# A gated attention and gMLP mixer on one core: w_phi loaded block-diagonal, and the first two tiles' matmuls by column halves

## The chip, the cores and the metric

The kernel runs on one core of a Trainium2 chip. The metric is device time in microseconds (us); lower is better. All times below are us unless marked ns. Engines are called by the profile's names: PE (TensorE matmul), PEld (its weight loads), DVE (VectorE), ACT (ScalarE), POOL (GpSimd) and SP (SyncE, which here only issues DMAs). A "q" behind a name (SPq, ACTq) is that engine's own queue of instructions that issue DMAs.

## What is computed

x is [2048, 512] in bf16. Two branches are mixed by a gate per row. Cut to what matters:

```python
g = sigmoid((x * gate_w).sum(-1, keepdims=True))
# branch A: linear attention, 32 heads of 16
q, k, v = split(x @ wqkv)
pq, pk = q @ w_phi[h], k @ w_phi[h]                     # per head, 16 x 16
phi = concat(softmax(p), softmax(-p))                   # for pq and pk
kv, z = phi_k.T @ v, phi_k.sum(0)                       # per head
a = ((phi_q @ kv) / (phi_q @ z + 1e-6)) @ wo
# branch B: gMLP
zz = gelu(x @ w_in)                                     # [2048, 1376]
z1, z2 = zz[:, :688], layernorm(zz[:, 688:])
b = (z1 * (w_sp @ z2 + b_sp[:, None])) @ w_out
out = g * a + (1 - g) * b
```

## The kernel before

Rows of x are handled in 16 tiles of 128. x transposed, xT, is the stationary operand of nearly all first-stage matmuls; its 512 rows are four blocks of 128, called dt = 0 to 3.

**The stages.** (1) For each tile, z2 = gelu(x @ w_in[:, 688:]) and z1 = gelu(x @ w_in[:, :688]): eight matmuls for each, four dt blocks by two column halves j of 344 (z_mm, L201; z_one, L193). z2_tile also makes the gate's logit: gate_w stands as one more column, column 688 of w_z2, so that half j=1 has 345 columns. z2_norm (L269) normalizes z2 four tiles at a time. The order by chunks c of four tiles is z2 of the chunk, then z1 of the chunk. In chunks c=2 and c=3 `fold` (L315) multiplies w_phi into the key part and the query part of wqkv; it reads wqkT (wqkv transposed) and wphi, a block-diagonal [128, 4, 128] image of w_phi with eight 16x16 heads to a 128-column block. (2) Then, tile by tile, keys, values, the kv sum, and w_sp @ z2 (gg_half, L460), with queries between them. (3) Attention output and the last products with wo and w_out (L500 to L505), and the stores.

**What sets the order.** PE and ACT run in the order in which the program is written (manual_schedule, L336). DVE, POOL and SP are ordered by the planner. Each engine takes its queue strictly in order. A DMA issue from SP or ACT is an instruction of that queue. The DMAs of both share eight completion marks in turn, so the ninth DMA in program order, and each one after it, is issued only when the DMA eight places earlier has landed.

**The start.** SP loads the rows of tiles 0 and 1 (xs, L122 and L124), block dt=2 of w_z2, and the rows of tiles 2 and 3 in one DMA (L129). ACT loads blocks dt=0 and dt=1 of w_z2, the gate row, and block dt=3. POOL issues the DMA of the bias row b_sp (brow, L118). Then SP issues w_z1 in two DMAs (L132), six DMA transposes of x for tiles 4 to 15 (L135, L137), w_phi into 16 partitions (wphiE, L140), the DMA transpose of the query and key parts of wqkv (L141), the value part (wv_sb, L142), and four DMA transposes of w_sp (L147).

`z2_first_two` (L219) writes out by hand what PE does first. It begins with matmuls of constants (warm_up, L224) into a buffer that is overwritten later. `x_T(i, d0, d1, ...)` (L282) transposes blocks of xs on PE into a PSUM buffer called pq, and DVE (or ACT) copies them to xT. `one(tt, dt, j)` is one z2 matmul of tile 0 or 1. `gate_T` (L292) turns the gate row into a column with one small matmul into a pq buffer, and a DVE copy puts it into w_z2's column 688; all matmuls of half j=1 wait for it. There are two pq buffers, taken in turn (pq_tile, L190), and three zp buffers (zp_tile, L187), in which z1 and z2 accumulate. `b_T` (L297) does with the bias row what gate_T does with the gate row; its result bT is first read by gg_half's DVE instruction (L468). `wphi_fold` (L302) builds wphi: four PE matmuls spread wphiE by the 0/1 matrix eexp, and DVE multiplies by the mask mask_bd. eexp and mask_bd are made on POOL (L151 to L164).

Of the kernel before, what the change touches and what calls it, by code (L numbers as in the profile page):

```python
# [8 lines left out]
ALU = mybir.AluOpType  # L9
AX = mybir.AxisListType  # L10
FP32 = mybir.dt.float32
BF16 = mybir.dt.bfloat16
I32 = mybir.dt.int32

P = 128
S = 2048
D = 512
H = 32
DH = 16
F = 1376  # L20
FH = 688
HF = FH // 2
NT = S // P
NDT = D // P
# [11 lines left out]
def kernel(  # L36
# [14 lines left out]
    nc = tc.nc  # L51
# [6 lines left out]
    early = early_cm.__enter__()  # L58
# [5 lines left out]
    w_z2 = early.tile([P, NDT, WP], BF16, name="w_z2")  # L64
    wv_sb = kvw.tile([P, NDT, D], BF16, name="wv_sb")
# [3 lines left out]
    z2all = pers.tile([P, NT, FH], BF16, name="z2all")  # L69
    z1all = pers.tile([P, NT, FH], BF16, name="z1all")  # L70
    wqkT = early.tile([P, 8, D], BF16, name="wqkT")
    wphiE = early.tile([P, H, DH], BF16, name="wphiE")
    eexp = early.tile([P, P], BF16, name="eexp")
    wphi = early.tile([P, NDT, P], BF16, name="wphi")
    mask_bd = early.tile([P, P], BF16, name="mask_bd")
    mask64 = pers.tile([P, NG, DH], BF16, name="mask64")
    mask4 = pers.tile([P, NG], BF16, name="mask4")
    kvz = pers.tile([P, 8, AW], BF16, name="kvz")
# [16 lines left out]
    gaterow = early.tile([P, P], BF16, name="gaterow")  # L95
    brow = early.tile([P, P], BF16, name="brow")
    zeros = early.tile([P, 32], BF16, name="zeros")

    w_in_v = B_w_in.rearrange("(dt p) f -> p dt f", p=P)
# [7 lines left out]
        out=ramp[:, 0, :], data0=ones32[:, :], data1=zeros[:, :], initial=0.0,  # L107
# [4 lines left out]
    for q in range(4):  # L112
        qs = slice(32 * q, 32 * q + 32)
        nc.vector.tensor_tensor(
            out=ident[qs, qs], in0=ramp[qs, 0, :], in1=ramp[qs, 1, :], op=ALU.is_equal)
    nc.gpsimd.memset(brow[:], 0.0)
    nc.gpsimd.memset(wphiE[:], 0.0)
    nc.gpsimd.dma_start(out=brow[0:NT, :], in_=B_b_sp.rearrange("(t p) -> t p", p=P))  # L118
    def load_z2w(eng, dt):
        eng.dma_start(out=w_z2[:, dt, 0:FH], in_=w_in_v[:, dt, FH:F])  # L120

    nc.sync.dma_start(out=xs[:, 0, :], in_=x2[0:P, :])  # L122
    load_z2w(nc.scalar, 0)
    nc.sync.dma_start(out=xs[:, 1, :], in_=x2[P:2 * P, :])  # L124
    load_z2w(nc.scalar, 1)
    load_z2w(nc.sync, 2)
    nc.scalar.dma_start(out=gaterow[0:NDT, :], in_=gate_w.rearrange("(dt p) -> dt p", p=P))
    load_z2w(nc.scalar, 3)
    nc.sync.dma_start(  # L129
        out=xs[:, 2:4, :], in_=x2[2 * P:4 * P, :].rearrange("(i p) d -> p i d", p=P))  # L130
    for h in range(2):
        nc.sync.dma_start(  # L132
            out=w_z1[:, 2 * h:2 * h + 2, :], in_=w_in_v[:, 2 * h:2 * h + 2, 0:FH])
    for i in range(4, 8):
        nc.sync.dma_start_transpose(out=xT[:, :, i * P:(i + 1) * P], in_=x2[i * P:(i + 1) * P, :])  # L135
    for q in range(2, NCH):
        nc.sync.dma_start_transpose(  # L137
            out=xT[:, :, q * CH:(q + 1) * CH], in_=x2[q * CH:(q + 1) * CH, :]
        )
    nc.sync.dma_start(out=wphiE[0:DH, :, :], in_=A_w_phi.rearrange("h e f -> e h f"))  # L140
    nc.sync.dma_start_transpose(out=wqkT[:, :, :], in_=A_wqkv[:, 0:2 * D])  # L141
    nc.sync.dma_start(  # L142
        out=wv_sb[:, :, :],
        in_=A_wqkv[:, 2 * D:3 * D].rearrange("(dt p) n -> p dt n", p=P),
    )
    for q in range(NCH):
        nc.sync.dma_start_transpose(  # L147
            out=wspT[:, :, q * CH:(q + 1) * CH], in_=B_w_sp[q * CH:(q + 1) * CH, :]
        )
    nc.gpsimd.memset(mhalf[:], -0.5)  # L150
    nc.gpsimd.memset(eexp[:], 0.0)  # L151
    nc.gpsimd.affine_select(
        out=eexp[:, :], in_=eexp[:, :], pattern=[[0, 8], [-1, 16]],
        compare_op=ALU.not_equal, fill=1.0, base=0, channel_multiplier=1,
    )
    nc.gpsimd.memset(mask_bd[:], 1.0)
    nc.gpsimd.affine_select(
        out=mask_bd[:], in_=mask_bd[:], pattern=[[-16, 8], [0, 16]],
        compare_op=ALU.is_ge, fill=0.0, base=0, channel_multiplier=1,
    )  # L160
    nc.gpsimd.affine_select(
        out=mask_bd[:], in_=mask_bd[:], pattern=[[16, 8], [0, 16]],
        compare_op=ALU.is_ge, fill=0.0, base=15, channel_multiplier=-1,
    )  # L164
    nc.gpsimd.memset(mask4[:], 1.0)
    nc.gpsimd.affine_select(
        out=mask4[:], in_=mask4[:], pattern=[[-32, NG]],
        compare_op=ALU.is_ge, fill=0.0, base=0, channel_multiplier=1,
    )
    nc.gpsimd.affine_select(  # L170
        out=mask4[:], in_=mask4[:], pattern=[[32, NG]],
        compare_op=ALU.is_ge, fill=0.0, base=31, channel_multiplier=-1,
# [17 lines left out]
    def pq_tile(shape, dtype=FP32):  # L190
        return psF.tile(shape, dtype, name="pq", tag=next_turn("pq", 2))
# [16 lines left out]
    def z2_out(tt, zp):  # L208
        z2v = z2all[:, tt, :].rearrange("p (j n) -> p j n", j=2)
        nc.scalar.activation(out=z2v, in_=zp[:, :, 0:HF], func=AF.Gelu_apprx_tanh)  # L210
        nc.vector.tensor_copy(out=glog[:, tt:tt + 1], in_=zp[:, 1, HF:HF + 1])
        for j in range(2):
            nc.vector.bn_stats(out=bn6[:, tt, j, :], in_=z2v[:, j, :])  # L213
        nc.vector.bn_aggr(out=mv[:, tt, :], in_=bn6[:, tt, :, :].rearrange("p j s -> p (j s)"))
# [4 lines left out]
    def z2_first_two():  # L219
        zps = [zp_tile() for _ in range(2)]  # L220
        tp1 = psA.tile([P, 2, P], BF16, name="tp1", tag=next_turn("zp", 3))
        turn["zp"] -= 1

        def warm_up(n, w=CH):  # L224
            for _ in range(n):
                nc.tensor.matmul(
                    zps[0][:, 1, 0:w], lhsT=nc.const_aps.tensor(1.0, [P, P], BF16),
                    rhs=nc.const_aps.tensor(1.0, [P, w], BF16), start=True, stop=True)

        def one(tt, dt, j):  # L230
            z_one(zps[tt], tt, w_z2, FH + 1, dt, j)

        warm_up(6)
        warm_up(5, P)
        x_T(0, 0, 1, pq_tile([P, 1, P], BF16)[:, :, :])
        x_T(0, 1, NDT, pq_tile([P, 3, P], BF16)[:, :, :], on_act=True)
        warm_up(3, P)
        one(0, 0, 0)
        x_T(1, 0, 2, tp1[:, :, :])
        x_T(1, 2, NDT, pq_tile([P, 2, P], BF16)[:, :, :], on_act=True)  # L240
        one(0, 1, 0)
        warm_up(2, P)
        one(1, 0, 0)
        one(1, 1, 0)
        gate_T()
        one(0, 2, 0)
        one(1, 2, 0)
        for dt in range(2):
            one(0, dt, 1)
            one(1, dt, 1)  # L250
        one(0, 2, 1)
        one(1, 2, 1)
        x_T(2, 0, NDT, pq_tile([P, NDT, P], BF16)[:, :, :])
        one(0, 3, 0)
        one(0, 3, 1)
        z2_out(0, zps[0])
        one(1, 3, 0)
        one(1, 3, 1)
        z2_out(1, zps[1])
        x_T(3, 0, NDT, pq_tile([P, NDT, P], BF16)[:, :, :])  # L260

    def z1_tile(tt):
        zp = z_mm(tt, w_z1, FH)
# [18 lines left out]
    def x_T(i, d0, d1, tp, on_act=False):  # L282
        for dt in range(d0, d1):
            nc.tensor.transpose(tp[:, dt - d0, :], xs[:, i, dt * P:(dt + 1) * P], ident[:, :])  # L284
        dst = xT[:, d0:d1, i * P:(i + 1) * P]
        if on_act:
            nc.scalar.copy(out=dst, in_=tp)
        else:
            with tc.high_priority():
                nc.vector.tensor_copy(out=dst, in_=tp)  # L290

    def gate_T():  # L292
        gt = pq_tile([P, NDT])
        nc.tensor.matmul(gt[:, :], lhsT=gaterow[:, :], rhs=ident[:, 0:NDT], start=True, stop=True)
        nc.vector.tensor_copy(out=w_z2[:, :, FH], in_=gt[:, :])

    def b_T():  # L297
        bt = pq_tile([P, NT])
        nc.tensor.matmul(bt[:, :], lhsT=brow[:, :], rhs=ident[:, 0:NT], start=True, stop=True)
        nc.vector.tensor_copy(out=bT[:, :], in_=bt[:, :])  # L300

    def wphi_fold():  # L302
        wps = pq_tile([P, NDT, P])
        for kc in range(NDT):
            nc.tensor.matmul(
                wps[:, kc, :], lhsT=eexp[:, :],
                rhs=wphiE[:, kc * 8:(kc + 1) * 8, :].rearrange("e h f -> e (h f)"),
                start=True, stop=True,
            )
        nc.vector.tensor_tensor(  # L310
            out=wphi[:, :, :], in0=wps[:, :, :],
            in1=mask_bd[:, None, :].to_broadcast([P, NDT, P]), op=ALU.mult,
        )

    def fold(qk):  # L315
        dst = (wq_p if qk == 0 else wk_p)[:].rearrange("p dt n -> p (dt n)").rearrange(
            "p (m r f) -> p r m f", r=4, f=32)
# [18 lines left out]
    with tc.manual_schedule(engines={mybir.EngineType.PE, mybir.EngineType.Activation}):  # L336
        z2_first_two()
        z2_tile(2)
        z2_tile(3)
        b_T()  # L340
        for c in range(NCH):
            ts = list(range(c * 4, c * 4 + 4))
            for tt in ts:
                if c > 0:
                    z2_tile(tt)
                if c >= 2 and tt % 4 == 1:
                    later = fold(3 - c)
            for tt in ts:
                z1_tile(tt)
                if c >= 2 and tt % 2 == 0:  # L350
                    later.pop(0)()
            z2_norm(ts)
            if c == 1:
                wphi_fold()

    psA_cm.__exit__(None, None, None)
    psF_cm.__exit__(None, None, None)
# [261 lines left out]
```

The softmax here doesn't subtract the row's maximum and nothing guards it: scores larger than these inputs give would overflow.

## Time and profile before

| what | us |
|---|---|
| median of 9 runs | 208.57 (208.25 to 208.88) |
| the profiled execution, its own time | 208.69 |
| its span (first to last instruction in the trace) | 206.9 |
| PE busy in the span | 202.3 |
| PE waits for block dt=2 of w_z2, once | 0.75 |
| z2_tile(2), the first tile after z2_first_two, starts at | 8.61 |
| first fold starts at | 27.64 |
| first matmul that reads the transposed w_sp | 48.0 |

The span begins with the first instruction that the profiler records, and all times of the trace count from there. The 1.8 between the execution's own time and its span lie outside what the trace shows. In a row of the timeline the first number is the start, the second the time from the first start to the last end of the merged instructions; matmuls are pipelined, so a group's time is longer than what one more of them adds. In brackets stands how long the engine had been idle and what released it.

The rate of the DMA queues over the first four of the page's 40 slices (5.17 each) is 181, 279, 147 and 244 GB/s.

### The profile page before, as it was taken

The numbers are of one execution on the slowest core, as the hardware profiler recorded it, in microseconds if no ns is written. First come the engines' busy times: TensorE is split into PE (matmuls) and PEld (weight loads), VectorE is DVE, ScalarE is ACT, GpSimd is POOL, SyncE is SP. The second block draws the span as 40 slices with busy tenths as digits, with TensorE's granted clock in tenths as the row PEclk, the third lists the DMA queues.
The fourth block names the chain that finished last, engine by engine and source line by source line (L and its number), as shares of the span: only waits on it lengthen the run. The fifth ranks groups of instructions, "written<-read, shape, count | busy, mean of one in ns | idle before, by whom it ended". The sixth has DMA issues, their size and how long they took to land.

```text
span 206.9 us, 3967 instructions
## 1 busy us (share of the span) xinstructions
PE 202.3 (98%) x1552; PEld 120.7 (58%) x1552; DVE 129.0 (62%) x278; ACT 77.0 (37%) x124; POOL 46.4 (22%) x78
## 2 busy tenths in 40 slices
PE   8899999999999999999999999999999999999994
PEld 4566666665566555556565666555455555665642
DVE  3477766655977776879797788555466553633330
ACT  3666668786322233333323032222251126002322
POOL 7020202020532327244242422222204220200000
PEclk9999999999999999999999999999999999999999
DMA  6999999999933015971413229856656567553442
GB/s 181 279 147 244 236 290 217 240 271 249 231 75 40 3 38 113 313 109 22 89 31 61 51 38 118 151 108 63 116 150 67 101 111 182 62 104 68 127 89 78
DMA packets 88971, 27.22 MB, mean 132 GB/s; under 512 B 82968, under 2 KB 88952, under 8 KB 88952
## 3 DMA queue, kind: packets, MB, share of 16 engines
q1 hardware_dynamic: 86176, 24.37, 61.9%
q10 hardware_dynamic: 2744, 2.60, 3.9%
q8 instruction: 12, 0.20, 0.4%
q14 instruction: 7, 0.06, 0.1%
q0 software_dynamic: 32, 0.00, 0.0%
HBM read 4.41 MB, written 2.10 MB: 31 GB/s over the span
## 4 chain that ended last, share of the span: by engine, by line
PE 95%; DMA 2%; SPq 0%; DVE 0%; issue 0%
PE mm L463 36%; PE zp L195 18%; PE mm L372 14%; PE mm L502 8%; PE mm L500 7%; PE mm L412 7%; DMA w_z<-in_B_w_in_dram 2%; PE at L476 2%; PE kvacc L428 2%; PE mm L505 1%; PE zp L324 0%; PE pq L284 0%; SPq L124 0%; SPq L122 0%; PE pq L324 0%; DVE ob L512 0%
## 5 line engine op out<-in xcount | busy, mean ns | idle before, releaser
L463 PE MATMUL mm<-z2all,wspT 128*128 128x344 bf16 x512 | 79.9, 309 | 0.0
L463 PEld LDWEIGHTS <-wspT 128*128 128x128 bf16 x512 | 49.0, 98 | 25.7 <-issue 0.4
L195 PE MATMUL zp<-w_z,xT 128*128 128x344 bf16 (+1 forms) x256 | 38.9, 309 | 0.8 <-DMA w_z<-in_B_w_in_dram 0.8
L376 ACT ACTIVATE eq<-mm 128x512 bf16<-128x512 f32 x32 | 17.4, 594 | 51.3 <-PE mm L372 25.6
L380 DVE TENSOR_REDUCE zs<-eq 128x64 f32<-128x1024 bf16 x16 | 19.5, 1220 | 20.3 <-ACT eq L376 20.3
L195 PEld LDWEIGHTS <-xT 128*128 128x128 bf16 x256 | 24.6, 98 | 12.8 <-issue 0.8
L468 DVE SCALAR_TENSOR_TENSOR ucat<-mm,bT,z1all 128x344 bf16<-128x344 f32 x32 | 17.4, 544 | 21.9 <-PE mm L463 21.9
L389 POOL TENSOR_TENSOR eq<-eq,ratio 128x512 bf16<-128x512 bf16 x16 | 16.9, 1055 | 50.2 <-DVE ratio L388 41.8
L376 ACT ACTIVATE ek<-mm 128x512 bf16<-128x512 f32 x32 | 17.3, 601 | 27.2 <-PE mm L372 27.2
L516 ACT ACTIVATE ob<-mm,g_inv 128x512 bf16<-128x512 f32 (+1 forms) x16 | 10.9, 680 | 32.8 <-PE mm L505 28.3
L380 DVE TENSOR_REDUCE zs<-ek 128x64 f32<-128x1024 bf16 x16 | 19.3, 1209 | 2.8 <-ACT ek L376 2.8
L502 PE MATMUL mm<-wspT,uT 128*128 128x512 bf16 (+2 forms) x85 | 20.1, 366 | 0.0
L372 PEld LDWEIGHTS <-xT 128*128 128x128 bf16 x128 | 12.2, 98 | 13.0 <-PE mm L505 0.8
L389 POOL TENSOR_TENSOR ek<-ek,ratio 128x512 bf16<-128x512 bf16 x16 | 16.9, 1056 | 2.0 <-DVE ratio L388 1.2
L500 PE MATMUL mm<-wspT,oT 128*128 128x512 bf16 (+2 forms) x68 | 16.6, 366 | 0.0
L372 PE MATMUL mm<-wq_p,xT 128*128 128x512 bf16 x64 | 16.4, 379 | 0.0
L412 PE MATMUL mm<-wv_sb,xT 128*128 128x512 bf16 x64 | 16.4, 379 | 0.0
L372 PE MATMUL mm<-wk_p,xT 128*128 128x512 bf16 x64 | 16.4, 379 | 0.0
L213 DVE BATCH_NORM_STATS2 bn<-z2all 128x6 f32<-128x344 bf16 x32 | 14.9, 502 | 0.0
L210 ACT ACTIVATE z2all<-zp 128x688 bf16<-128x688 f32 x16 | 11.8, 743 | 7.3 <-PE zp L195 6.9
L264 ACT ACTIVATE z1all<-zp 128x688 bf16<-128x688 f32 x16 | 11.9, 743 | 5.1 <-PE zp L195 5.1
L502 PEld LDWEIGHTS <-uT 128*128 128x128 bf16 x85 | 8.1, 98 | 9.2
(80 smaller groups left out, 146.5 us busy)
## 6 DMA issues: line engine op xcount, KB each, us to landing
out_dram<-ob ACTq DMA_DIRECT2D x15, 128.0 KB, 1.8
wspT<-in_B_w_out_dram SPq DMA_DIRECT2D x2, 640.0 KB, 5.3
w_z<-in_B_w_in_dram SPq DMA_DIRECT2D x2, 344.0 KB, 4.8
w_z<-in_B_w_in_dram ACTq DMA_DIRECT2D x3, 172.0 KB, 3.2
wv_sb<-in_A_wqkv_dram SPq DMA_DIRECT2D x1, 512.0 KB, 4.8
wspT<-in_A_wo_dram SPq DMA_DIRECT2D x1, 512.0 KB, 5.0
xs<-in_A_x_dram SPq DMA_DIRECT2D x2, 128.0 KB, 2.8
xs<-in_A_x_dram SPq DMA_DIRECT2D x1, 256.0 KB, 5.2
```

The source lines that it names most:

```text
L195: nc.tensor.matmul(zp[:, j, 0:n], lhsT=xT[:, dt, tt * P:(tt + 1) * P], rhs=wt[:, dt, j * HF:j * HF + n], start=(dt == 0), stop=(dt == NDT ...
L213: nc.vector.bn_stats(out=bn6[:, tt, j, :], in_=z2v[:, j, :])
L264: nc.scalar.activation(out=z1all[:, tt, :].rearrange("p (j n) -> p j n", j=2), in_=zp[:, :, 0:HF], func=AF.Gelu_apprx_tanh,)
L372: nc.tensor.matmul(ps[:, :], lhsT=xT[:, dt, tt * P:(tt + 1) * P], rhs=w[:, dt, :], start=(dt == 0), stop=(dt == NDT - 1))
L376: nc.scalar.activation(out=e[:, :, a, :], in_=ps[:, :].rearrange("p (h f) -> p h f", f=DH), func=AF.Exp, scale=1.0 - 2.0 * a)
L380: nc.vector.tensor_reduce(out=z[:].rearrange("p h a -> p (h a)"), in_=e[:].rearrange("p h a f -> p (h a) f"), axis=AX.X, op=ALU.add,)
L389: nc.gpsimd.tensor_tensor(out=e[:, :, 1, :], in0=e[:, :, 1, :], in1=ratio[:, :, None].to_broadcast([P, H, DH]), op=ALU.mult)
L412: nc.tensor.matmul(v_ps[:, :], lhsT=xT[:, dt, tt * P:(tt + 1) * P], rhs=wv_sb[:, dt, :], start=(dt == 0), stop=(dt == NDT - 1))
L463: nc.tensor.matmul(gp[:, 0:HF], lhsT=wspT[:, st, tt * P:(tt + 1) * P], rhs=z2all[:, st, j * HF:(j + 1) * HF], start=(st == 0), stop=(st == ...
L468: nc.vector.scalar_tensor_tensor(out=ucat[tt % NU][:, c0 + j * HF:c0 + (j + 1) * HF], in0=gp[:, 0:HF], scalar=bT[:, tt:tt + 1], in1=z1all[ ...
L500: nc.tensor.matmul(acc, lhsT=oT[:, g, :], rhs=wo_t[:, g, c0:c1], start=(g == 0), stop=False)
L502: nc.tensor.matmul(acc, lhsT=uT[:, i + ft, :], rhs=w_main[i][:, ft, c0:c1], start=False, stop=False)
```

## The change

It has five parts.

1. wphi is loaded block-diagonal at once: it is cleared on POOL, and eight DMAs on SP, one for each place u in a block of eight heads, put 16 partitions x 4 blocks x 16 elements on the diagonal. wphiE, eexp, mask_bd and wphi_fold go. These DMAs stand behind the DMA transposes of wqkv.
2. The bias row's DMA moves from POOL to SP, behind the transposes of x, and b_T moves from behind z2_tile(3) to the end of chunk c=1, the place of wphi_fold.
3. Block dt=0 of w_z2 is loaded in two column halves on ACT; the gate row moves from ACT to SP, behind the rows of tiles 2 and 3, where it is the ninth DMA in program order.
4. The DMA transpose of wqkv becomes two, the key part first, and the load of wv_sb becomes two.
5. In z2_first_two, tiles 0 and 1 do half j=0 for all four dt first, then come x_T(2), gate_T and x_T(3), then half j=1, tile by tile. Four small warm-up matmuls go.

```diff
-    nc.gpsimd.memset(wphiE[:], 0.0)
-    nc.gpsimd.dma_start(out=brow[0:NT, :], in_=B_b_sp.rearrange("(t p) -> t p", p=P))
+    nc.gpsimd.memset(wphi[:], 0.0)
...
     nc.sync.dma_start(out=xs[:, 0, :], in_=x2[0:P, :])
-    load_z2w(nc.scalar, 0)
+    nc.scalar.dma_start(out=w_z2[:, 0, 0:HF], in_=w_in_v[:, 0, FH:FH + HF])
     nc.sync.dma_start(out=xs[:, 1, :], in_=x2[P:2 * P, :])
+    nc.scalar.dma_start(out=w_z2[:, 0, HF:FH], in_=w_in_v[:, 0, FH + HF:F])
+    load_z2w(nc.sync, 2)
     load_z2w(nc.scalar, 1)
-    load_z2w(nc.sync, 2)
-    nc.scalar.dma_start(out=gaterow[0:NDT, :], in_=gate_w.rearrange("(dt p) -> dt p", p=P))
-    load_z2w(nc.scalar, 3)
     nc.sync.dma_start(
         out=xs[:, 2:4, :], in_=x2[2 * P:4 * P, :].rearrange("(i p) d -> p i d", p=P))
+    load_z2w(nc.scalar, 3)
+    nc.sync.dma_start(out=gaterow[0:NDT, :], in_=gate_w.rearrange("(dt p) -> dt p", p=P))
...
-    nc.sync.dma_start(out=wphiE[0:DH, :, :], in_=A_w_phi.rearrange("h e f -> e h f"))
-    nc.sync.dma_start_transpose(out=wqkT[:, :, :], in_=A_wqkv[:, 0:2 * D])
-    nc.sync.dma_start(
-        out=wv_sb[:, :, :],
-        in_=A_wqkv[:, 2 * D:3 * D].rearrange("(dt p) n -> p dt n", p=P),
-    )
+    nc.sync.dma_start(out=brow[0:NT, :], in_=B_b_sp.rearrange("(t p) -> t p", p=P))
+    for qk in (1, 0):
+        nc.sync.dma_start_transpose(
+            out=wqkT[:, qk * NDT:(qk + 1) * NDT, :], in_=A_wqkv[:, qk * D:(qk + 1) * D])
+    heads = A_w_phi.rearrange("(kc u) e f -> u e kc f", u=8)
+    for u in range(8):
+        us = slice(u * DH, (u + 1) * DH)
+        nc.sync.dma_start(out=wphi[us, :, us], in_=heads[u])
+    for h in range(2):
+        nc.sync.dma_start(
+            out=wv_sb[:, 2 * h:2 * h + 2, :],
+            in_=A_wqkv[h * 2 * P:(h + 1) * 2 * P, 2 * D:3 * D].rearrange("(dt p) n -> p dt n", p=P),
+        )
...
         warm_up(6)
-        warm_up(5, P)
+        warm_up(2, P)
...
         one(0, 1, 0)
-        warm_up(2, P)
+        warm_up(1, P)
         one(1, 0, 0)
         one(1, 1, 0)
+        for dt in range(2, NDT):
+            one(0, dt, 0)
+            one(1, dt, 0)
+        x_T(2, 0, NDT, pq_tile([P, NDT, P], BF16)[:, :, :])
         gate_T()
-        one(0, 2, 0)
-        one(1, 2, 0)
-        for dt in range(2):
-            one(0, dt, 1)
-            one(1, dt, 1)
-        one(0, 2, 1)
-        one(1, 2, 1)
-        x_T(2, 0, NDT, pq_tile([P, NDT, P], BF16)[:, :, :])
-        one(0, 3, 0)
-        one(0, 3, 1)
-        z2_out(0, zps[0])
-        one(1, 3, 0)
-        one(1, 3, 1)
-        z2_out(1, zps[1])
         x_T(3, 0, NDT, pq_tile([P, NDT, P], BF16)[:, :, :])
+        for tt in range(2):
+            for dt in range(NDT):
+                one(tt, dt, 1)
+            z2_out(tt, zps[tt])
...
-        b_T()
         for c in range(NCH):
...
             if c == 1:
-                wphi_fold()
+                b_T()
```

The removed eexp and mask_bd set-up on POOL, and the function wphi_fold itself, are left out of this cut.

More of the change, by code (lines that the diff above doesn't have):

```diff
@@ L71 @@
     wqkT = early.tile([P, 8, D], BF16, name="wqkT")
-    wphiE = early.tile([P, H, DH], BF16, name="wphiE")
-    eexp = early.tile([P, P], BF16, name="eexp")
     wphi = early.tile([P, NDT, P], BF16, name="wphi")
-    mask_bd = early.tile([P, P], BF16, name="mask_bd")
     mask64 = pers.tile([P, NG, DH], BF16, name="mask64")
@@ L150 @@
     nc.gpsimd.memset(mhalf[:], -0.5)
[L151 to L164, printed above, removed]
     nc.gpsimd.memset(mask4[:], 1.0)
@@ L300, in b_T @@
         nc.vector.tensor_copy(out=bT[:, :], in_=bt[:, :])
[L302 to L313, printed above, removed]
     def fold(qk):
```

## The prediction

> **What bounds the kernel now.** I read three views in this order. First the page's shares and its chain that ended last: they say which engine sets the end.
>
> ```profile
> PE 202.3 (98%) x1552; PEld 120.7 (58%) x1552; DVE 129.0 (62%) x278; ACT 77.0 (37%) x124; POOL 46.4 (22%) x78
> PE 95%; DMA 2%; SPq 0%; DVE 0%; issue 0%
> ```
>
> TensorE (PE) is the bound from the first matmuls to the last store. So a delay or gain on PE's stream near the start shifts everything behind it, and other engines count only where PE waits for them. Second, the chain in order of time, its start:
>
> ```profile
> 1.74 4.62 DMA w_z<-in_B_w_in_dram
> 6.37 0.04 issue
> 6.41 1.33 PE zp L195 x8
> 7.74 0.22 PE pq L284 x4
> 7.96 0.59 PE zp L195 x4
> 8.55 0.22 PE pq L284 x4
> 8.77 2.34 PE zp L195 x16
> ...
> 25.15 0.22 PE pq L305 x4
> ```
>
> The columns are start, us, what. PE stands until block dt=2 of w_z2 lands at 6.36; from 6.41 it runs without a gap (a 344-column matmul costs 2.34/16 = 0.146, four transposes 0.22). Third, the timeline around the hand-over to tile 2:
>
> ```profile
> 6.41 1.33 PE L195 MATMUL zp<-w_z,xT 128*128 128x344 bf16 x8 [0.75 <-DMA w_z<-in_B_w_in_dram]
> 7.58 0.39 PE L284 MATMUL pq<-ident,xs 128*128 128x128 bf16 x4
> 7.80 0.75 PE L195 MATMUL zp<-w_z,xT 128*128 128x344 bf16 x4
> 8.00 0.42 DVE L290 COPY xT<-pq 128x512 bf16<-128x512 bf16 x1 [2.10 <-PE pq L284]
> 8.38 0.39 PE L284 MATMUL pq<-ident,xs 128*128 128x128 bf16 x4
> 8.61 2.50 PE L195 MATMUL zp<-w_z,xT 128*128 128x344 bf16 x16
> ```
>
> At 8.61 z2_tile(2) starts: the mark that I carry to the changed kernel. Between the two sets of transposes lie four matmuls, and under them VectorE's 0.42 copy of the first set. Landings, from the DMA issues in short windows (issue plus time to landing): dt=2 1.74+4.62 = 6.36, dt=3 2.36+4.5 = 6.86, xs rows of tiles 2 and 3 2.21+5.2 = 7.41.
>
> **The start, step by step.** After the change the same twelve matmuls follow dt=2, in another order: four of column half 0 (two with dt=2, two with dt=3), then x_T(2), gate_T, x_T(3), then eight of half 1.
>
> Ahead of 6.41 nothing counts while dt=2 is late: three small warm-ups and one more are gone, dt=0 comes in halves and dt=1 is issued one issue (about 0.45) later; 4.5 (1.27+3.2) becomes 4.95 at worst, and the four matmuls before the wait are then through by about 5.5. If that cover were gone, the warm-ups would be worth some 0.3 and the late dt=1 cost 0.2.
>
> dt=2, dt=3 and the xs rows keep their places: same number of issues ahead of them on each queue, dt=3 about 0.2 earlier. With their landings unchanged, the two dt=2 matmuls run 6.41 to 6.70, dt=3 holds the next two from 6.70 to 6.90, they end at 7.20, and x_T(2) waits for its rows until 7.45. Before, eight matmuls stood in that place and both waits fell under them.
>
> Then a new wait. psF has two "pq" buffers taken in turn. Before, x_T(3) got the buffer of gate_T, long free. Now gate_T stands between x_T(2) and x_T(3), so x_T(3) gets x_T(2)'s buffer and must wait for the VectorE copy: from the rows, first transpose 7.58 to copy end 8.42 is 0.84, plus 0.06 to the next PE start (copy 4.09+0.22, matmul 4.37). PE's own work in that time is four transposes and the gate matmul, 0.24, so 0.66 is idle. Calling x_T(2)'s start s: x_T(3) starts at s+0.90, half 1 at s+1.13 (gate's 0.18 cast follows the copy on VectorE, done by about s+1.04), and after 8 x 0.146 = 1.17 z2_tile(2) starts at s+2.30. Queued behind this wait on PE is all that follows; ScalarE's Gelu and VectorE's statistics move with it, and their buffers (zp turns) come free as far ahead of need as before.
>
> The gate row, now fifth on SP, is issued when the first half of dt=0 has landed (at most 3.7) and moves behind the xs rows in SP's queue. It must be there by about s+0.5; between xs (7.41) and the first w_z1 half (3.75+4.5 = 8.25) it costs 0 to 0.35. I take 0, its neighbour being xs.
>
> s hangs on the xs landing. Unchanged: 7.45. Early side: from 4.0 to 5.0 the DMA rate falls to 249 and 219 GB/s against some 360 around it, in the microsecond in which the small bias and gate rows are on the queues; they leave it. Worth (360-234) x 1 us = 0.13 MB, or 0.35 us. Late side: the half rows are twice as many packets; the row for a 128x1376-byte block gives no price for 688-byte ones, and I bound it by one more 172 KB block at 360 GB/s, 0.5. I take half of the early side: s = 7.3, so z2_tile(2) at 9.60, **0.99 later**.
>
> The trace's landing marks show the xs rows landing in 16 parts: 14 of them by 6.58, the last two at 6.99 and 7.35. [...]
>
> **w_phi.** wphi_fold goes: 0.22 on the chain (25.15), **0.22 saved**. Its VectorE mask multiply (0.69 at 25.50) was needed only by the fold at 27.64, and POOL's memsets and selects end by 4.6 with POOL idle until 13.5: off the path, nothing. b_T's matmul costs 0.01 before (11.11) and after. In its place come eight DMAs on SP. Rows of SP's queue:
>
> ```profile
> 13.94 1.38 SPq L140 DMA_DIRECT2D wphiE<-in_A_w_phi_dram  x1
> 15.37 4.69 SPq L141 DMA_TRANSPOSE wqkT<-in_A_wqkv_dram  x1
> 20.10 0.58 SPq L142 DMA_DIRECT2D wv_sb<-in_A_wqkv_dram  x1
> 20.73 34.31 SPq L147 DMA_TRANSPOSE wspT<-in_B_w_sp_dram  x4
> ```
>
> Now brow (about 0.45) and the wqkT halves come first, from 14.3 to 19.2; then eight issues between 0.41 (a 128-row block) and 0.57 (the 4-row gate) each, 3.3 to 4.6 in all, to 22.5 to 23.8. wphiE landed 4.4-1.38 = 3.0 after its issue ended, so the last block lands at 25.5 to 26.8. The fold needs it at 27.64+0.77 = 28.4: covered by 1.6 to 2.9. Upper bound: each at wphiE's 1.38, 11 in all, landing at 33: a stall of 4.8. wv then goes out as two issues (about 1) and the wspT transposes start at about 24, 3 us later than 20.73: the first (12.1 to landing) is there by 37 and needed at 48, the last issue ends near 58 and lands before 65, first read by tile 12, past 129. The uT transposes behind them (56.43) move by some 3, and are first read by L502 near 130. All hidden.
>
> [...]
>
> **Sum.** +0.99 - 0.22 = **+0.77**. The profiled execution took 208.69, its span 206.9 with 1.8 around it (left as it is): 208.69+0.77 = 209.46. The median of the nine runs is 208.57, so 209.34 there; I state **209.4**. In general the net is s - 6.53.
>
> **Rivals.** About 0.2% (0.42) is what a measurement of this kernel can tell from no change; that is s within 6.11 to 6.95.
> - *Forecast*, s 7.1 to 7.6: +0.57 to +1.07. Chance 0.50.
> - *Earlier landings*, s 6.55 to 7.1, the dip at 4 to 5 us mostly gone: 0 to +0.57. Chance 0.22, of which 0.05 still slower and 0.17 no change. For it: the dip. Against it: packets of dt=2, dt=3 and xs themselves begin there.
> - *Faster*: the transfers land 1.3 or more earlier, together, so that x_T(2) follows its matmuls without a wait. Place: the SP and ACT queues from 2.5 to 6; it decides at s = 6.11. Bound: the seven transfers are 1,200 KB (1.23 MB), at 360 GB/s from 2.5 on done at 5.9; s = 6.0 gives -0.53, 208.1. Against it: then even the buffer wait of 0.66 stays. Chance 0.15, 0.08 of it no change and 0.07 faster.
> - *A new late transfer*: w_phi's blocks at the fold (+0.8 to +5.5) or half rows that slow dt=2 (+1.1 to +1.4). Chance 0.08.
> - *Around the span*: with no GpSimd DMA left, some of the 1.8 outside the span goes, up to 1: 208.3. No row speaks for it. Chance 0.05, faster.
>
> Slower 0.50+0.05+0.08 = 0.63, no change 0.17+0.08 = 0.25, faster 0.07+0.05 = 0.12. The range: down to s about 6.3 (208.3) and up to the late xs, s = 7.95 (7.45+0.5: +1.42, 210.1).
>
> **What would show it.** PE idle some 0.66 between gate_T and x_T(3), released by VectorE's xT copy; PE idle before dt=3 and before x_T(2), released by DMAs; z2_tile(2) near 9.6; no wait at the first fold; no L305. The forecast is wrong if the xs rows land before 6.9, or if PE waits for wphi.

## The result and the profile after

The changed kernel is slower: the ratio to the kernel before is 1.0076, 95% interval 1.0055 to 1.0097, from runs side by side. On before's median of 208.45 (43 runs) that is +1.58 (1.15 to 2.02). Six of the 13 executions, 212.6 to 213.1 and so more than 1.5% above the fastest, are left out of that ratio, and none of them was profiled; the median of all 13 is 211.78. Of the seven that count, five took 209.3 to 209.8 and two took 211.07 and 211.78. The profiled execution is one of the first group: 209.38, span 207.7, so +0.69 and +0.8 against the one of before.

The page's first lines, as for the kernel before:

```profile
PE 201.9 (97%) x1544; PEld 120.4 (58%) x1544; DVE 129.3 (62%) x277; ACT 77.0 (37%) x124; POOL 44.6 (21%) x72
```

PE is still the bound: 0.4 less work in a span that is 0.8 longer. The start of the chain in order of time:

```profile
1.74 4.52 DMA w_z<-in_B_w_in_dram
6.26 0.04 issue
6.30 0.31 PE zp L185
6.61 0.06 PE zp L216
6.66 0.87 PE zp L185 x6
7.54 0.22 PE pq L268 x4
7.76 0.05 PE pq L278
7.81 0.42 DVE xT L274
8.23 0.04 issue
8.28 0.38 PE pq L268 x4
8.66 4.39 PE zp L185 x30
```

The one DMA in the chain is now block dt=1, ACT's third load: it lands at 6.26, not at the 4.5 of before, and PE stands 1.56 for it: the first matmul with dt=1 holds up all that is written behind it. Then x_T(2) (start 7.37), gate_T, the VectorE copy as the new link, x_T(3) after a wait of 0.51, and half 1 from 8.49. From the timeline:

```profile
6.30 0.31 PE L185 MATMUL zp<-w_z,xT 128*128 128x344 bf16 x1 [1.56 <-DMA w_z<-in_B_w_in_dram]
8.28 0.38 PE L268 MATMUL pq<-ident,xs 128*128 128x128 bf16 x4 [0.51 <-DVE xT L274]
```

Block dt=2 (1.74+4.3 = 6.04) and the xs rows (2.20+5.1 = 7.3) landed in time for their matmuls, and PE waits for no other load. Eight matmuls at 0.146 later, at 9.66, z2_tile(2) starts; before it was 8.61. So **+1.05** at that mark.

The first fold starts at 28.48 (27.64 before), +0.84: wphi_fold's share is gone. Then 0.15 comes back at the end of the first stage. The chain there:

```profile
39.17 5.96 PE zp L185 x40
...
45.16 0.74 ACT z1all L248
45.90 0.48 ACT wq_p L302
46.39 0.04 issue
46.43 1.67 PE mm L342 x7
```

The key matmuls (L342) wait for ScalarE's last copy of the query fold; PE's last z1 matmul ended near 46.28. Before, the chain ran from z1 to the key matmuls (L372) without a gap, at 45.45. From there the shift stays at 1.0 down to the last store, whose landing is 0.2 shorter in this execution. The eight w_phi issues took 4.03 (19.79 to 23.82) and landed 2.0 after their issue; the fold waits for none. The wspT transposes begin at 24.84 and nothing waits for them.

### The profile page after: what moved, and what is told of

Its sections match the earlier page's. It is cut to its first block, busy times and chain, and to the rows that moved or that the text cites. A ratio compares the mean times of both kernels' runs of the same rounds, so it can differ in the third digit from the quotient of the medians.

```text
span 207.7 us, 3964 instructions
## 1 busy us (share of the span) xinstructions
PE 201.9 (97%) x1544; PEld 120.4 (58%) x1544; DVE 129.3 (62%) x277; ACT 77.0 (37%) x124; POOL 44.6 (21%) x72
## 4 chain that ended last, share of the span: by engine, by line
PE 95%; DMA 2%; ACT 1%; ACTq 0%; DVE 0%; issue 0%
PE mm L433 36%; PE zp L185 18%; PE mm L342 14%; PE mm L472 8%; PE mm L470 7%; PE mm L382 7%; DMA w_z<-in_B_w_in_dram 2%; PE at L446 2%; PE kvacc L398 2%; PE mm L475 1%; PE zp L295 0%; ACT z1all L248 0%; PE pq L268 0%; ACT wq_p L302 0%; ACTq L121 0%; DVE xT L274 0%
## 5 line engine op out<-in xcount | busy, mean ns | idle before, releaser
L185 PE MATMUL zp<-w_z,xT 128*128 128x344 bf16 (+1 forms) x256 | 38.3, 309 | 1.6 <-DMA w_z<-in_B_w_in_dram 1.6
L342 PEld LDWEIGHTS <-xT 128*128 128x128 bf16 x128 | 12.2, 98 | 13.2 <-PE mm L475 0.8
L342 PE MATMUL mm<-wq_p,xT 128*128 128x512 bf16 x64 | 16.4, 379 | 0.0
L342 PE MATMUL mm<-wk_p,xT 128*128 128x512 bf16 x64 | 16.3, 379 | 0.1
```

The costliest lines, as they stand in the source:

```text
L185: nc.tensor.matmul(zp[:, j, 0:n], lhsT=xT[:, dt, tt * P:(tt + 1) * P], rhs=wt[:, dt, j * HF:j * HF + n], start=(dt == 0), stop=(dt == NDT ...
L342: nc.tensor.matmul(ps[:, :], lhsT=xT[:, dt, tt * P:(tt + 1) * P], rhs=w[:, dt, :], start=(dt == 0), stop=(dt == NDT - 1))
```

## The experiments

Ratios are to the kernel before, run side by side on the same chip, with 95% intervals; us are medians. "Mark" is the start of z2_tile(2) in the profiled execution (8.61 before, 9.66 after).

| run | kernel | us (range) | ratio | mark |
|---|---|---|---|---|
| e1_wphi_only | parts 1, 2, 4 | 208.17 (207.79 to 208.63) | 0.9981 (0.9967 to 0.9994) | 8.17 |
| e2_start_only | parts 3, 5 | 211.9 (210.15 to 213.32) | 1.0129 (1.0088 to 1.017) | 12.3 |
| e3_free_buffer | after, x_T(3) in another buffer | 211.15 (209.72 to 211.6) | 1.0118 (1.009 to 1.0146) | 10.0 |
| e4_turn | after, one pq turn skipped | 211.09 (209.33 to 212.54) | 1.0092 (1.0058 to 1.0125) | 12.7 |
| e5_wphi_turn | e1, one pq turn skipped | 208.07 (207.66 to 208.69) | 0.9976 (0.9961 to 0.9991) | 8.13 |
| e6_whole_dt0 | after, dt=0 in one DMA | 208.98 (208.51 to 209.72) | 1.0015 (0.9999 to 1.003) | 9.08 |
| e7_busy_waits | after, waits filled | 210.2 (209.87 to 210.33) | 1.0065 (1.0045 to 1.0084) | 10.45 |
| e8_bias_only | before, part 2 alone | 208.13 (207.86 to 208.5) | 0.9973 (0.9957 to 0.9989) | 8.00 |
| e9_half_last | after, second half of dt=0 last | 209.49 (209.14 to 210.21) | 1.0046 (1.003 to 1.0062) | 9.63 |
| e10_fewer_warm | before, four warm-ups fewer | 208.65 (207.93 to 209.84) | 1.0005 (0.9986 to 1.0024) | 8.53 |

My first theory was that of the prediction: the loss is made in the first ten microseconds, by the order of the matmuls and the buffer wait. The rival was the longer SP queue.

**e1 and e2: each half of the change alone.** e1 takes the diff's parts 1, 2 and 4, e2 its parts 3 and 5.

> Before with only the w_phi blocks, the late bias row and the split wqkv and wv loads (parts 1, 2 and 4); the start as before. My theory, that the loss is made in the first ten microseconds: z2_tile(2) starts at 8.6 as before, the 0.22 of wphi_fold goes, and some 0.14 comes back where the first key matmul waits for the last query fold copy (the pq buffers fall the other way round): 208.4, no change. The rival, that the longer SP queue costs the time (small blocks late at the fold, or w_sp and uT transposes late): about 0.8 slower, 209.3, with a PE wait between 25 and 60.

> Before with only the start changed (parts 3 and 5: dt=0 in halves, gate row on SP, matmuls by column halves); wphi_fold and the bias row as before. My theory: z2_tile(2) starts near 9.65, the whole 1.05 later, and all of it reaches the end: 209.5. The rival (SP queue): within 0.2 of before.

The SP queue costs nothing: e1 is a little faster than before. The loss is all in the start: e2 loses no less than the whole change (1.0129 against 1.0076; the intervals just overlap). But both sizes are off. e1 gained at a place that I had not credited to it: z2_tile(2) at 8.17, with no wait for dt=2. And e2 lost more than the 1.05: dt=1 landed at 7.58 (1.75+5.83), later still than in the whole change, PE stood 2.38 for it, and then ran at half its clock. This is the granted clock in e2 (stretch, its length, then the busy time of PE, PEld, DVE, ACT and POOL, PEclk, DMA share, GB/s), for the stretch of 3.41 at half clock and one of that length on either side:

```profile
5.56:8.98 3.42, 1.36 (x13) 1.02 (x13) 0.00 (x0) 1.37 (x2) 0.00 (x0) 1.00 1.45 314
8.98:12.39 3.41, 2.90 (x16) 1.73 (x14) 1.15 (x5) 0.74 (x1) 0.00 (x0) 0.50 0.88 136
12.39:15.80 3.41, 3.41 (x26) 2.27 (x25) 3.25 (x14) 2.23 (x3) 0.00 (x0) 1.00 1.00 222
```

The wait makes a stretch in which PE is busy for 1.36 of 3.42; in the next one PEclk is 0.50, and then full again. A matmul of half 1 adds 0.293 there (PEclk 0.50) and 0.146 in the changed kernel (PEclk 1.00). PE is busy for 2.90 of that stretch, so my estimate of its cost is half of that, 1.45; in a stretch with PE busy throughout it would be half of 3.41, 1.7. And e2's mark is 3.7 later than before's (half 1 from 9.97, eight matmuls at 0.293: 12.3). Two stretches of the same length in the profiled execution of the changed kernel:

```profile
3.91:7.32 3.41, 1.85 (x19) 1.28 (x18) 0.52 (x2) 2.22 (x4) 0.00 (x0) 1.00 1.01 309
7.32:10.73 3.41, 2.90 (x27) 2.10 (x26) 1.57 (x6) 1.38 (x2) 0.00 (x0) 1.00 1.33 234
```

PE is busy for 1.85 of 3.41 in the first of them, and PEclk is 1.00 in both. So a new theory: the late dt=1 makes the wait, and in some executions the wait costs clock as well. The two executions of the changed kernel at 211.07 and 211.78 have a mean granted clock of 0.992 and 0.991 over their spans of 209.3 and 210.0: 0.008 x 209.3 = 1.7, which fits one stretch such as e2's; neither of the two was profiled.

**e3 and e4: the buffer wait, and the turn of the buffers.**

```diff
-        x_T(3, 0, NDT, pq_tile([P, NDT, P], BF16)[:, :, :])
+        tp3 = psA.tile([P, NDT, P], BF16, name="tp3", tag=next_turn("zp", 3))
+        turn["zp"] -= 1
+        next_turn("pq", 2)
+        x_T(3, 0, NDT, tp3[:, :, :])
```

> The changed kernel, but x_T(3) writes to the free zp buffer, so that it need not wait for the copy of x_T(2); the turn of the pq buffers afterwards is kept. My theory: the 0.5 wait ahead of x_T(3) goes, z2_tile(2) starts near 9.15, 0.5 faster than the changed kernel, some 0.35 above before. The rival, that the late transfers alone make the loss and that the buffer wait only takes over time lost anyway (the gate column, for one, would hold half 1): less than 0.15 gained, a wait for the gate column in its place.

The rival holds. From e3's timeline:

```profile
8.28 0.41 DVE L277 COPY xT<-tp 128x512 bf16<-128x512 bf16 x1
8.61 0.17 DVE L282 CAST w_z<-pq 128x4 bf16<-128x4 f32 x1
8.83 2.36 PE L185 MATMUL zp<-w_z,xT 128*128 128x345 bf16 x15 [0.68 <-DVE w_z L282]
```

x_T(3) no longer waits, but its copy now stands ahead of gate's cast on VectorE, and half 1 waits 0.68 for the cast. Freeing one buffer moved the wait.

e4 is the changed kernel with `next_turn("pq", 2)` behind b_T in chunk 1.

> The changed kernel with one turn of the pq buffers skipped behind b_T, so that the folds get their buffers as in the kernel before. My theory: the gap of 0.14 between the last z1 matmul and the first key matmul goes, 0.14 faster than the changed kernel. Rival: the gap has another cause (the copy of the query fold is simply later) and stays; no difference.

Its executions are too far apart to show 0.14 in the time. The gap is settled by its trace, in which the key matmuls follow the last z1 matmuls at 49.61 without a gap, and by e5, which has the same line.

**e5 and e8: where e1's gain comes from.** e5 is e1 with the skipped turn; e8 is the kernel before with only the bias row's DMA and b_T moved:

```diff
-    nc.gpsimd.dma_start(out=brow[0:NT, :], in_=B_b_sp.rearrange("(t p) -> t p", p=P))
...
+    nc.sync.dma_start(out=brow[0:NT, :], in_=B_b_sp.rearrange("(t p) -> t p", p=P))
     nc.sync.dma_start(out=wphiE[0:DH, :, :], in_=A_w_phi.rearrange("h e f -> e h f"))
```

> Parts 1, 2 and 4 on the old start (as e1), and one turn of the pq buffers skipped behind b_T. My theory: the 0.15 gap ahead of the first key matmul, seen in e1 and in the changed kernel and gone in e4, goes here too: 0.15 faster than e1, 0.5 to 0.6 faster than before, 208.0. Rival (gap goes but something else waits, as the key matmul then stands at the next copy): same as e1.

> Before with the bias row alone moved (part 2): its DMA from POOL at 1.4 to SP behind the transposes of x, b_T to the end of chunk 1. Theory A, that the small DMA from POOL held up the loads of the start: dt=2 lands near 5.7 and the xs rows of tiles 2 and 3 near 6.7, as in e1, the 0.75 wait goes, 0.4 faster than before. Theory B, that e1 gained by wphi_fold's 0.22 alone and its early landings were chance: dt=2 lands near 6.3 and the time is that of before, within 0.1.

The gap goes with the turn. In e5 the chain runs from the last z1 matmuls straight on:

```profile
37.64 7.11 PE zp L184 x48
44.76 1.86 PE mm L348 x8
```

In the trace that is worth 0.15; in the medians e5 (208.07) and e1 (208.17) differ by less than their intervals tell apart. So the gap's cause is the pq turn: wphi_fold was one turn, and without it the folds' last two copies fall to the other two buffers.

e8 gains 0.27% (0.11 to 0.43) with the bias row alone. From its DMA issues in a window and its timeline:

```profile
xs<-in_A_x_dram SPq DMA_DIRECT2D x1, 256.0 KB, 4.6
w_z<-in_B_w_in_dram SPq DMA_DIRECT2D x1, 172.0 KB, 4.0
```

```profile
5.78 1.34 PE L195 MATMUL zp<-w_z,xT 128*128 128x344 bf16 x8
8.00 4.25 PE L195 MATMUL zp<-w_z,xT 128*128 128x344 bf16 x28
```

dt=2 lands at 1.75+4.0 = 5.75 (6.36 before) and the xs rows at 2.22+4.6 = 6.8 (7.41 before); PE's 0.75 wait is gone and the mark is 8.00. So in this pair of executions the loads land 0.6 earlier without the one 4 KB DMA issued from POOL at 1.4. The size varies from one execution to the next: e10 has that DMA and lands dt=2 at 1.74+4.2 = 5.94 and the xs rows at 2.21+4.9 = 7.1, only 0.2 and 0.3 later than e8; e1 and e5, without it, land the xs rows at 6.6 and 6.4. Each of the two with the DMA is later than each of the three without it. e1, e5 and e8 beat both kernels, and are not told apart: the w_phi part by itself is worth nothing that these runs can show.

**e6 and e9: the halves of dt=0.** e6 loads dt=0 whole again in the changed kernel; e9 keeps the halves and moves one issue:

```diff
-    nc.scalar.dma_start(out=w_z2[:, 0, HF:FH], in_=w_in_v[:, 0, FH + HF:F])
...
     load_z2w(nc.scalar, 3)
+    nc.scalar.dma_start(out=w_z2[:, 0, HF:FH], in_=w_in_v[:, 0, FH + HF:F])
```

> The changed kernel with block dt=0 loaded in one DMA again. Theory A, that the halves make the late landing (dt=1 is one issue later, and the queues carry twice the packets for dt=0): dt=1 lands near 5.0 instead of 6.3 and dt=2 near 5.7, the PE wait there shrinks from 1.56 to about 0.5 and x_T(2) starts near 6.8; the clock is granted at once more often, and the executions come within 0.3 of before. Theory B, that the late landing comes from moving the gate row or from chance: dt=1 or dt=2 still lands after 6.0 and the executions spread as those of the changed kernel do, 209.4 to 213.

> The changed kernel with the second half of dt=0 issued last on ACT, behind dt=3 (half 1 reads it only after 8.4). Theory A, that dt=1 is late because the second half stands ahead of it on ACT's queue: dt=1 lands at 5.3 or before, x_T(2) starts near 7, the time comes to that of e6_whole_dt0, within 0.3 of before. Theory B, that halves as such (rows of 688 bytes, one DMA more) slow the queues: dt=1 or dt=2 lands after 6.0 still, and executions spread to 211 and beyond.

e6: theory A. PE does not wait for dt=1 or dt=2 at all, x_T(2) starts at 6.77, the mark is 9.08, and the 12 executions lie within 1.2 of each other, 0.15% above before:

```profile
6.77 0.40 PE L267 MATMUL pq<-ident,xs 128*128 128x128 bf16 x4
```

e9 splits theory A in two. dt=1 lands at 1.24+3.4 = 4.64 and the executions come together, so its lateness was its place behind the second half. But x_T(2) does not start near 7, and the time does not come to e6's. From its timeline:

```profile
6.12 0.85 PE L185 MATMUL zp<-w_z,xT 128*128 128x344 bf16 x4 [0.49 <-DMA w_z<-in_B_w_in_dram]
7.33 0.40 PE L268 MATMUL pq<-ident,xs 128*128 128x128 bf16 x4 [0.36 <-DMA xs<-in_A_x_dram]
```

dt=2 and the xs rows still land at about 6.0 and 7.3 and PE waits for both: these are two of the waits that the prediction carried, for dt=2 and for xs, in plain sight; one for dt=3 is not there. With dt=0 whole (e6) the xs rows land at 2.2+4.5 = 6.7 and dt=2 at 1.73+4.2 = 5.93. So in these executions the xs rows pay some 0.6 for the halves wherever the second one stands, and dt=2 only 0.1; the ratios, 1.0046 and 1.0015, differ by 0.31%. Why was not tried apart: packets of 688 bytes, one transfer more, or the gate row, which is the ninth DMA in e9 and goes out at 3.48, and the eighth in e6, where it goes out at 2.68.

**e7 and e10: the clock.** e7 adds small matmuls of constants, extra work that the reference does not need: `warm_up(13, P)` ahead of `one(0, 1, 0)` and `warm_up(7, P)` behind gate_T. e10 takes only the four warm-ups out of the kernel before.

> The changed kernel with 20 more small matmuls of constants, 13 ahead of the wait for dt=1 and 7 between gate_T and x_T(3): extra work in time in which PE stands idle. Theory A, that the granted clock falls to half in one or two windows of 3.41 because PE is idle too much in the first ten microseconds, each costing 1.7: with the waits filled the executions lie close together at 209.3 to 209.8, none near 211.5 or 213. Theory B, that the spread comes from the transfers themselves landing late in some executions: the spread stays, and each execution is at best as fast as now, or 0.3 slower by the added matmuls.

> Before with only the four small warm-up matmuls removed that the change removes. Theory A, that the clock falls because of the long waits: as before within 0.2, no execution above 209.9. Theory B, that the removed warm-ups alone leave PE too idle for the full clock: some executions near 210.3 or 212, one or two windows of 1.7 more.

e7's six executions lie within 0.46 of each other, 209.87 to 210.33, where the changed kernel's seven that count span 2.5. They lie 0.1 to 0.5 above the upper end of what I expected: in the profiled one dt=1 landed at 7.04, and PE waited 0.96 for it even after the 13 matmuls:

```profile
7.08 0.31 PE L185 MATMUL zp<-w_z,xT 128*128 128x344 bf16 x1 [0.96 <-DMA w_z<-in_B_w_in_dram]
```

So transfers as late as this, with PE kept busy beside them, did not bring the times of 211 and more back, which speaks for the idle PE. e7 ran on another chip than e1 to e4, and the changed kernel was not run beside it, so a difference between chips is not excluded. e10 is the same as before within its interval, so the four warm-ups by themselves are not the cause. Its executions are somewhat further apart (207.93 to 209.84), which I leave open.

The granted clock does not tell all. In e4's profiled execution (212.54) PEclk is 9 in all 40 slices and the mean clock is 1.00; yet six matmuls that add 0.87 to the changed kernel's chain (6.66) add twice that:

```profile
7.34 1.72 PE zp L185 x6
```

At that pace, 0.29 each, it also does half 1. On a smaller scale, the first z2 matmul of tile 0 takes 0.49 in e10 and 0.32 in the kernel before, both with PEclk at 1.00. So at the start of these traces a PEclk of 1.00 does not show full pace; what one matmul adds does. e3's executions at 211.0 to 211.6, with a mean clock of 1.00, may have lost time this way; none of them was profiled, and it is not shown.

## Why the prediction was right, and where not

- **Direction, and the mark.** Slower was right. z2_tile(2) was forecast for 9.60 and came at 9.66; x_T(2) for 7.3, and came at 7.37. That agreement is partly luck, as the next two points show.
- **The landings.** I kept dt=2, dt=3 and the xs rows near their old landings, with half of the bias row's effect as a gain. Two larger effects cancelled. The bias row is worth 0.6 at the mark (e8: 8.61 to 8.00; 0.2 to 0.6 by landings), so the rival of earlier landings was a true effect. With the bias row alone gone, the xs rows land at 6.8 (e8), and at 6.6 in e1, which is without it too: nearer to the 6.6 or so by which 14 of their 16 parts had landed before than to my 7.3. The halves take it back (e6 to the change: 9.08 to 9.66, 0.58).
- **dt=1, the step that failed.** "4.5 becomes 4.95 at worst" counted only one issue more. It landed at 6.26 in the profiled execution, at 7.04 and 7.58 in e7 and e2. The wait that I had hidden under dt=2 became the one that ends last. e9 shows that its place behind the second half was the reason: moved ahead of that half, it landed at 4.64. The late side for the halves, 0.5, was put on xs only. Of the signs that I named, the buffer wait, the mark, the quiet first fold and the missing L305 came; PE's waits before dt=3 and before x_T(2) did not, because dt=1's wait covered them.
- **The buffer wait.** From x_T(2) to x_T(3) 0.90 was forecast and 0.91 came, released by the VectorE copy as forecast. Of it 0.51 is idle, not 0.66: by the trace the transposes and the gate matmul last 0.40 (7.37 to 7.77), where I counted 0.24. As a term it stands; as a cause it does not stand alone, since the gate cast sits right behind it (e3). The order's price with dt=1 and dt=2 in time is e6 against e8, 1.08 at the mark, from one execution of each. In e6 x_T(2) starts right behind the landing of its rows (6.7), as forecast.
- **w_phi.** wphi_fold's 0.22 came (1.05 at the mark, 0.84 at the fold). The blocks were forecast out by 22.5 to 23.8 and were out at 23.82, no wait at the fold. The eight landed 2.0 after their issue (median), one under the other's issue, and all eight issues took 4.03. Missed: the turn of the pq buffers, +0.15 (e5).
- **The sum.** +0.77 forecast; +0.69 and a span of +0.8 in the profiled execution.
- **The size.** The ratio says +1.58, the sum's double, and my working had no term for the difference. One part of it is the granted clock. I read PEclk at 9 in all slices of the kernel before and did not ask what a longer wait would do to it. The five executions at 209.3 to 209.8 average 209.57, +1.1 on before's median; the two at 211.07 and 211.78, with their clock of 0.99, lift the average of the seven to 210.1. The page's slices show 9 after the change too, since the profiled execution is one of the five. The five's own +1.1 is 0.4 more than the profiled execution shows, and that stays unexplained; single executions of one kernel lie that far apart.
- **Around the span.** 1.8 before and 1.7 after: that rival did not happen.

## What to carry to other kernels

Price a load that is split in two by what stands behind it on its queue, not by its own landing: the next block paid 1.6 here (6.26 against 4.64 in e9). The half that is needed late belongs last (1.0046 in e9 against 1.0076), and the block left whole did better still (1.0015 in e6). A wait at the start can have a second price: in e2 PE was busy for 1.36 of 3.42, and the granted clock was 0.50 for the next 3.41. So look at several executions before trusting one profile, and in the profile at what one matmul adds at the start (0.29 instead of 0.146 in e4), not at the granted clock alone. And when a helper that takes a buffer from a rotation is removed, count the turns: everything behind it changes buffers (0.15 here).

## What the runs showed of the hardware

- With a 4 KB DMA from POOL at 1.4 the big loads of SP land 0.2 to 0.6 later: dt=2 at 6.36 (before) and 5.94 (e10), against 5.75 without it (e8), and the xs rows at 7.41 and 7.1, against 6.8. No run here shows why.
- In e2 the granted clock is 0.50 from 8.98 to 12.39, which is 3.41, and 1.00 in the 3.42 ahead of it and the 3.41 behind it. PE was busy for 1.36 of the 3.42 ahead. In the changed kernel's profiled execution, with PE busy for 1.85 of 3.41, the clock was 1.00 in that stretch and the next. That the idle time brings the clock down is my theory; e7, with the waits filled and all six executions at 209.87 to 210.33, fits it.
- At the start a trace can show a granted clock of 1.00 while a 344-column matmul adds 0.29 instead of 0.146 (e4).
